# Chunks 4 to 15 of the first FFN layer as one stage for the first three units, with another order of weight loads

## The chip, the cores and the metric

One core of a Trainium2 chip. The metric is device time in microseconds (us), the median of several runs of the whole kernel. Each run holds attention and two feed-forward layers.

## The reference, cut to what matters

Attention runs over 4 batches, 8 heads, 576 positions and head size 64, with a mask in blocks of 64. Its output is regrouped to 2304 tokens of 512 numbers, and two feed-forward layers follow:

```python
def _moe_ref(x, w_in, w_out, alpha):            # layer 1, w_in 512 x 2048, w_out 2048 x 512
    h = x @ w_in
    g = np.maximum(h, 0.0) + alpha * np.minimum(h, 0.0)
    return (g @ w_out).astype(np.float32)

def _moe2_ref(x, w_in, w_out):                  # layer 2
    h = x @ w_in
    g = np.where(h > 0.0, h, np.exp(np.minimum(h, 0.0)) - 1.0)
    return (g @ w_out).astype(np.float32)
```

The kernel is handed the weights as 64-bit numbers and makes 32-bit ones of them itself.

## The kernel before, in words

**Units and chunks.** The 2304 tokens are cut into five units: units 0 to 3 have 512 tokens, unit 4 has 256 (`UNITS`). The 2048 hidden features are 16 chunks f of 128. One step of a feed-forward layer is one unit with one chunk: `l1_h` (line 537) or `l2_h` (588) forms h with 12 matmuls (4 slices of the 512 inputs, times three products of high and low parts), the gate makes g and splits it into two parts, and `l1_y` (634) or `l2_y` (614) multiplies by `w_out` with 12 more. `l1_y` and `l2_y` run three steps behind (`lag = 3`), so between them the gate has three steps' time. `l1_y` adds into four PSUM banks m = 0 to 3 over a unit's chunks; five banks serve in turn (`ring("acc", ...)`).

**Stages.** A unit's chunks of layer 1 need not run in one go. During attention, units 0 to 2 do chunks 0 to 3 (`l1_beside`, 551), and their partial sums z go to memory (`zd`). Behind attention, the list `units` (720) gives the order: stage A does chunks 0 to 7 of units 3 and 4 and writes z; stage B does chunks 4 to 7 of units 0, 1 and 2, loads z, adds and writes it again; stage D does chunks 8 to 15 of all five units, loads z, adds, splits the sum and writes it as y (`yd`). Stage C is layer 2, all 16 chunks of each unit. A3 is unit 3 in stage A, and so on; a hand-over is the end of one unit's `l1_y` and the start of the next one's. Each stage entry loads the unit's x (`load_x1`, 504) unless the unit stays the same (B2 to D2). Stages A, B, D and C have 16, 12, 40 and 80 steps; step 0 starts at 264.4 us, and stage B starts with step 16, D with 28, C with 68.

**Weights.** A chunk's weights are two words of 512 KB, r = 0 for `w_in` and r = 1 for `w_out`. `load_w` (112) loads one into a raw buffer (2 of them) from SyncE's queue and decodes it in a chain: ScalarE (lines 127, 128), VectorE (132, 133, 137), GpSimd (142), ScalarE (152), VectorE (83, called from 145). `later` and `end_tick` (two ticks a step) set the place of each link in the order of the text: the first link comes `arrival` ticks behind the load. `w_at` (729) says at which step each word is asked for. Decoded weights live in three pools: four slots for chunks 0 to 3, four for 4 to 7, eight for 8 to 15; layer 2 takes the slots of layer 1 when their last reader is done.

**What sets the order.** In attention the order of all engines is the text's. Behind it only TensorE's is (`tc.manual_schedule(engines={ET.PE})`, line 710). The queues of ScalarE, VectorE, GpSimd and SyncE are ordered by the framework's planner on a timeline of its own (`schedule_with_timeline_sim=True`), with the order of the text as rank: an instruction can come earlier than it stands if its operands and its buffer are free there. On the chip each queue then runs in that order.

**Buffers for g and y.** `gs_tile` (511) takes turns between a pool of four (`gs`) and a late pool of four (`gsl`); a stage that writes y takes four tiles more from the same turns at each hand-over. `z_tile` (579) has two and two.

Of the kernel before, what the change touches and what calls it, by code (L numbers as in the profile page):

```python
# [10 lines left out]
F32R = mybir.dt.float32r  # L11
U32 = mybir.dt.uint32
I32 = mybir.dt.int32
AF = mybir.ActivationFunctionType
ALU = mybir.AluOpType
# [4 lines left out]
P = 128  # L20
B, H, S, D = 4, 8, 576, 64
NT, DM, DFF = 2304, 512, 2048
KC = DM // P
NF = DFF // P
FA = 4
# [11 lines left out]
def f32(ap):  # L37
    return ap.bitcast(F32)
# [3 lines left out]
def attention_moe_kernel(ctx: ExitStack, tc: tile.TileContext, qT, kT, v_a, v_b, w1, w2, alpha, out):  # L42
    nc = tc.nc
    pe, act, dve, pool_e = nc.tensor, nc.scalar, nc.vector, nc.gpsimd
# [4 lines left out]
    wraw_p = ctx.enter_context(pool("wraw", 2))  # L49
# [18 lines left out]
    def ring(name, *banks):  # L68
        rings[name] = list(banks)
# [9 lines left out]
    zd = [dram.tile([P, KC, n], F32, name=f"zd{u}") for u, n in enumerate(UNITS)]  # L79


    def low_part(eng, out, x, high):
        return {"v": dve, "p": pool_e}[eng].tensor_tensor(out=out, in0=x, in1=f32(high), op=ALU.subtract)  # L83
# [13 lines left out]
    def later(ticks, emit):  # L97
        due.setdefault(tick[0] + ticks, []).append(emit)
# [8 lines left out]
    late_pools = []  # L107
# [4 lines left out]
    def load_w(layer, f, r):  # L112
        if r == 0:
            wt[layer, f] = w_pools[min(f // 4, 2)].tile([P, 2, 2 * DM], F32R, tag="w", name="w")
        t = wt[layer, f]
        raw = wraw_p.tile([P, 2 * DM], U32, tag="wraw", name="wraw")
        nc.sync.dma_start(out=raw, in_=(w1, w2)[layer][f, :, r * DM:(r + 1) * DM].bitcast(U32))
        pairs = raw.rearrange("p (n t) -> p n t", t=2)
        low, high = pairs[:, :, 0], pairs[:, :, 1]
        units = low.bitcast(I32)  # L120
        hi, lo = (t[:, k, r * DM:(r + 1) * DM] for k in range(2))
        word = []

        def first():
            w = wraw_p.tile([P, DM], F32, tag="wword", name="wword")
            word.append(w)
            act.activation(out=w, in_=high.bitcast(F32), func=AF.Abs)  # L127
            act.activation(out=units, in_=low, func=AF.Copy, scale=2.0 ** -29)

        def bits():  # L130
            w, wi = word[0], word[0].bitcast(U32)
            dve.tensor_scalar(w, w, F64_MIN, F64_MAX, ALU.max, ALU.min)  # L132
            dve.tensor_scalar(wi, wi, 3, 0x3FFFFFF8, ALU.logical_shift_left, ALU.bitwise_and)  # L133

        def sign():
            wi = word[0].bitcast(U32)
            dve.scalar_tensor_tensor(  # L137
                out=wi, in0=high, scalar=0xC0000000, in1=wi, op0=ALU.bitwise_and, op1=ALU.bitwise_or)

        def rounded():  # L140
            w = word[0].bitcast(I32)
            pool_e.tensor_tensor(out=w, in0=w, in1=units, op=ALU.add)  # L142

        def last():
            low_part("v", lo, word[0], hi)
            ready.add((layer, f, r))
        lead = arrival[0]
        later(lead, first)
        later(lead + 1, bits)
        later(lead + 1, sign)  # L150
        later(lead + 2, rounded)
        later(lead + 3, lambda: act.copy(hi, word[0]))  # L152
        later(lead + 4, last)

    arrival = [2]
# [5 lines left out]
    def w_out(layer, f, part, lo, n):  # L161
        assert (layer, f, 1) in ready
        return wt[layer, f][:, part, DM + lo:DM + lo + n]
# [335 lines left out]

    CHUNKS = {"A": range(FA), "B": range(FA, 8), "D": range(8, NF), "C": range(NF)}

    def load_x1(u):
        x1[u] = t = xp.tile([P, 2, KC, UNITS[u]], F32R, tag="x1", name="x1")
# [5 lines left out]
    def gs_tile():  # L511
        turn[0] += 1
        if late_pools and turn[0] % 2:
            return late_pools[0].tile([P, 2, 512], F32R, tag="gsl", name="gsl", bufs=4)
        return gp.tile([P, 2, 512], F32R, tag="gs", name="gs", bufs=FA)

    def l1_gate(f, h, n, beside=False):

        neg = gp.tile([P, 512], F32, tag="neg", name="neg", bufs=1)[:, :n]
        g = gp.tile([P, 512], F32, tag="g", name="g", bufs=3)[:, :n]  # L520
        t = gs_tile()[:, :, :n]
        act.activation(out=neg, in_=h, func=AF.Relu, scale=-1.0)  # L522

        def gate():
            dve.scalar_tensor_tensor(out=g, in0=neg, scalar=beta[:, f:f + 1], in1=h, op0=ALU.mult, op1=ALU.add)  # L525
            return parts

        def parts():
            act.copy(t[:, 0, :], g)  # L529
            low_part("p", t[:, 1, :], g, t[:, 0, :])  # L530
        if beside:
            held.append(gate)
        else:
            later(1, gate())
        return t
# [10 lines left out]
    def to_z(u, m, acc):  # L546
        z = z_tile(m)[:, :UNITS[u]]
        copy("av"[m % 2], z, acc)
        nc.sync.dma_start(out=zd[u][:, m, :], in_=z)
# [29 lines left out]
    def z_tile(m):  # L579
        if m % 2 and late_pools:  # L580
            return late_pools[0].tile([P, 512], F32, tag="zl", name="zl", bufs=2)
        return gp.tile([P, 512], F32, tag="z", name="z", bufs=2)
# [26 lines left out]
    def acc_bank(m, first):  # L609
        if first:  # L610
            accs[m] = bank[take("acc")]
        return accs[m]
# [21 lines left out]
    def l1_y(kind, u, f, gs):  # L634
        n, first, last = UNITS[u], f == CHUNKS[kind][0], f == CHUNKS[kind][-1]
        if kind != "A" and first:
            for m in range(KC):
                zs[m] = z_tile(m)[:, :n]
                nc.sync.dma_start(out=zs[m], in_=zd[u][:, m, :])
        for m in range(KC):  # L640
            acc = acc_bank(m, first)[:, :n]
            for t, (wp_, gp_) in enumerate(PASSES):
                pe.matmul(acc, w_out(0, f, wp_, m * P, P), gs[:, gp_, :n],  # L643
                          start=first and t == 0, stop=last and t == 2)
            if last and kind == "A":
                to_z(u, m, acc)
            elif last:
                z = zs.pop(m)
                if kind == "B":
                    dve.tensor_tensor(out=z, in0=acc, in1=z, op=ALU.add)  # L650
                    nc.sync.dma_start(out=zd[u][:, m, :], in_=z)
                    continue
                ys = gs_tile()[:, :, :n]
                dve.tensor_tensor(out=z, in0=acc, in1=z, op=ALU.add)  # L654
                act.copy(ys[:, 0, :], z)
                low_part("vp"[m % 2], ys[:, 1, :], z, ys[:, 0, :])
                nc.sync.dma_start(out=yd[u][:, :, m, :], in_=f32(ys))
# [52 lines left out]
    with tc.manual_schedule(engines={ET.PE}):  # L710


        att.close()
        ps = ctx.enter_context(pool("ps_all", 1, space=PSUM))
        bank[:] = [ps.tile([P, 512], F32, name=f"bank{i}") for i in range(8)]
        w_pools.append(ctx.enter_context(pool("w2", NF - 8)))
        late_pools.append(ctx.enter_context(pool("late", 1)))
        ring("h", 5, 6, 7)
        ring("acc", *range(5))
        units = [("A", 3), ("A", 4)] + [("B", u) for u in range(3)] + [  # L720
            ("D", u) for u in (2, 4, 3, 0, 1)] + [("C", u) for u in (2, 3, 0, 1, 4)]
        fs = CHUNKS
        fs["A"] = range(8)
        steps = [(k, u, f) for k, u in units for f in fs[k]]
        first_of = {}
        for i, (k, u, f) in enumerate(steps):
            first_of.setdefault((k, u), i)
        lag = 3
        w_at = {}
        for i in range(16):  # L730
            f, r = divmod(i, 2)
            w_at[1 + i * 26 // 16] = 0, 8 + f, r
            w_at[first_of["D", 2] + 1 + 2 * i] = 1, f, r
            w_at[first_of["C", 2] - 4 + i] = 1, 8 + f, r
        gs = {}
        for i in range(len(steps) + lag):
            if i in w_at:
                load_w(*w_at[i])
            if i < len(steps):
                k, u, f = steps[i]  # L740
                if f == fs[k][1]:
                    n = units.index((k, u)) + 1
                    if n < len(units) and units[n] != ("D", u):
                        (load_x2 if units[n][0] == "C" else load_x1)(units[n][1])
                gs[i] = l2_h(u, f) if k == "C" else l1_gate(f, l1_h(u, f), UNITS[u])
            end_tick()
            if i >= lag:
                k, u, f = steps[i - lag]
                if k == "C":
                    l2_y(u, f, gs.pop(i - lag))  # L750
                else:
                    l1_y(k, u, f, gs.pop(i - lag))
            end_tick()
# [32 lines left out]
```

## Time and profile before

| | |
|---|---|
| median of 3 runs | 1022.64 us (1018.75 to 1023.74) |
| profiled execution, its own time | 1017.45 us |
| its span | 1015.7 us, granted clock 0.987 |
| TensorE busy | 963.5 us (95%), 5008 matmuls |
| VectorE, ScalarE, GpSimd busy | 543.4 (54%), 440.2 (43%), 337.5 us (33%) |
| moved by DMA | 116.25 MB; 64 loads of weights, median 4.1 us from issue to landing |

The profile shows one execution. In it, "busy" is the time in which an engine works on instructions; an idle time is named after what ended it. A row of the timeline merges neighbouring instructions of one kind, with the start of the first and the time to the end of the last, and the count. PE is TensorE, DVE VectorE, ACT ScalarE, POOL GpSimd, SPq SyncE's queue of DMA issues.

### The profile page before, as it was taken

The numbers are of one execution on the slowest core, as the hardware profiler recorded it, in microseconds if no ns is written. First come the engines' busy times: TensorE is split into PE (matmuls) and PEld (weight loads), VectorE is DVE, ScalarE is ACT, GpSimd is POOL, SyncE is SP. The second block draws the span as 40 slices with busy tenths as digits, with TensorE's granted clock in tenths as the row PEclk, the third lists the DMA queues.
The fourth block names the chain that finished last, engine by engine and source line by source line (L and its number), as shares of the span: only waits on it lengthen the run. The fifth ranks groups of instructions, "written<-read, shape, count | busy, mean of one in ns | idle before, by whom it ended". The sixth has DMA issues, their size and how long they took to land.

```text
span 1015.7 us, 13946 instructions
## 1 busy us (share of the span) xinstructions
PE 963.5 (95%) x5008; PEld 774.9 (76%) x5008; DVE 543.4 (54%) x1024; ACT 440.2 (43%) x985; POOL 337.5 (33%) x401
## 2 busy tenths in 40 slices
PE   6778999999997999899999999999999999999997
PEld 4456766766686877689888887888888888888896
DVE  5877667787477766743213378943333333333342
ACT  6876566776455553543323256422222222222222
POOL 4778575685354544443323353200000000000000
PEclk9999999999998999999999999999999999999999
DMA  6553433633537676564423275302102100200010
GB/s 210 164 198 136 156 86 107 219 93 122 196 106 226 194 236 217 171 200 161 149 83 125 90 234 185 114 1 84 41 1 84 42 1 1 81 3 0 1 43 21
DMA packets 61156, 116.25 MB, mean 114 GB/s; under 512 B 11552, under 2 KB 29984, under 8 KB 59936
## 3 DMA queue, kind: packets, MB, share of 16 engines
q1 hardware_dynamic: 60800, 115.11, 34.3%
q8 instruction: 39, 0.64, 0.3%
q10 hardware_dynamic: 288, 0.26, 0.1%
q14 instruction: 29, 0.24, 0.1%
HBM read 83.89 MB, written 31.46 MB: 114 GB/s over the span
## 4 chain that ended last, share of the span: by engine, by line
PE 68%; DVE 11%; DMA 9%; POOL 4%; ACT 4%; issue 2%; SPq 1%; POOLq 0%; ACTq 0%; DVEq 0%
PE bank L618 19%; PE bank L593 18%; PE bank L643 9%; PE bank L542 8%; DMA wraw<-w 6%; PE bank L417 3%; POOL wword L142 3%; PE bank L571 3%; DVE wword L137 2%; PE bank L357 2%; PE pair L270 2%; PE bank L560 2%; DVE wword L133 2%; DVE wword L132 2%; ACT wword L127 1%
## 5 line engine op out<-in xcount | busy, mean ns | idle before, releaser
L593 PE MATMUL bank<-x,w 128*128 128x512 f32 (+1 forms) x960 | 210.0, 368 | 0.0
L593 PEld LDWEIGHTS bank<-x,w 128*128 128x128 f32 x960 | 169.3, 188 | 31.2
L542 PE MATMUL bank<-x,w 128*128 128x512 f32 (+1 forms) x816 | 176.7, 367 | 1.3 <-DVE xtail L83 1.3
L542 PEld LDWEIGHTS bank<-x,w 128*128 128x128 f32 x816 | 142.7, 191 | 26.2 <-ACT xtail L423 1.4
L597 ACT ACTIVATE e<-bank 128x512 f32<-128x512 f32 (+1 forms) x80 | 44.4, 554 | 180.3 <-PE bank L593 180.3
L598 DVE TENSOR_SCALAR e<-e 128x512 f32<-128x512 f32 (+1 forms) x80 | 32.0, 400 | 168.2 <-ACT e L597 168.2
L142 POOL TENSOR_TENSOR wword<-wword,wraw 128x512 int32<-128x512 int32 x64 | 89.8, 1405 | 92.5 <-DVE wword L137 53.8
L525 DVE SCALAR_TENSOR_TENSOR g<-neg,beta,bank 128x512 f32<-128x512 f32 (+1 forms) x80 | 55.2, 689 | 100.2 <-ACT neg L522 98.9
L643 PE MATMUL bank<-gsl,w 128*128 128x512 f32 (+1 forms) x408 | 94.6, 379 | 13.7 <-ACT z L87 5.3
L618 PE MATMUL bank<-w,gsl 128*128 128x512 f32 x432 | 105.2, 390 | 0.8 <-DVE z L654 0.5
L618 PE MATMUL bank<-w,gs 128*128 128x512 f32 x432 | 104.6, 389 | 0.0
L90 POOL TENSOR_SCALAR p<-p,stat 128x128 f32<-128x128 f32 (+4 forms) x144 | 81.3, 579 | 53.9 <-DVE stat L328 43.4
L643 PEld LDWEIGHTS bank<-gsl,w 128*128 128x128 f32 x408 | 72.8, 196 | 30.0 <-DVE z L650 6.3
L618 PEld LDWEIGHTS bank<-w,gsl 128*128 128x128 f32 x432 | 80.4, 188 | 17.9 <-DVE z L654 1.0
L618 PEld LDWEIGHTS bank<-w,gs 128*128 128x128 f32 x432 | 80.6, 188 | 16.4
L319 ACT ACTIVATE p<-pair,stat 128x128 f32<-128x128 f32 (+4 forms) x144 | 78.3, 557 | 26.9 <-DVE stat L292 20.5
L643 PE MATMUL bank<-gs,w 128*128 128x512 f32 (+1 forms) x408 | 87.8, 364 | 0.0
L83 POOL TENSOR_TENSOR gs<-g,gs 128x512 fp32r<-128x512 f32 (+1 forms) x46 | 57.2, 1244 | 88.0 <-ACT gs L529 77.4
L643 PEld LDWEIGHTS bank<-gs,w 128*128 128x128 f32 x408 | 70.6, 189 | 12.2
L83 DVE TENSOR_TENSOR w<-wword,w 128x512 fp32r<-128x512 f32 x64 | 61.0, 957 | 24.5 <-ACT w L152 23.7
L522 ACT ACTIVATE neg<-bank 128x512 f32<-128x512 f32 (+1 forms) x80 | 44.2, 552 | 68.2 <-PE bank L542 67.0
L292 DVE TENSOR_REDUCE stat<-pair 128x2 f32<-128x256 f32 (+3 forms) x80 | 63.2, 806 | 5.9 <-PE pair L275 3.8
(82 smaller groups left out, 1256.1 us busy)
## 6 DMA issues: line engine op xcount, KB each, us to landing
wraw<-w SPq DMA_DIRECT2D x64, 512.0 KB, 4.1
x<-xd SPq DMA_DIRECT2D x24, 512.0 KB, 7.7
xd<-x SPq DMA_DIRECT2D x4, 2048.0 KB, 8.7
x<-yd SPq DMA_DIRECT2D x4, 2048.0 KB, 8.3
vraw<-v_a SPq DMA_DIRECT2D x24, 256.0 KB, 3.6
zd<-z SPq DMA_DIRECT2D x20, 256.0 KB, 3.2
kraw<-kT SPq DMA_DIRECT2D x16, 288.0 KB, 4.3
yd<-gs SPq DMA_DIRECT2D x8, 512.0 KB, 3.2
```

The source lines that it names most:

```text
L83: return {"v": dve, "p": pool_e}[eng].tensor_tensor(out=out, in0=x, in1=f32(high), op=ALU.subtract)
L90: return pool_e.tensor_scalar(out, x, 1.0 if scale is None else scale, 1.0, ALU.mult, ALU.mult)
L142: pool_e.tensor_tensor(out=w, in0=w, in1=units, op=ALU.add)
L292: peak = lambda out, x, axis=AX.X: dve.tensor_reduce(out=out, in_=x, axis=axis, op=ALU.max, negate=True)
L319: act.activation(out=out, in_=x, func=AF.Exp, bias=stat[:, k:k + 1], accum_out=stat[:, SUMS + 2 * k:SUMS + 2 * k + 1])
L522: act.activation(out=neg, in_=h, func=AF.Relu, scale=-1.0)
L525: dve.scalar_tensor_tensor(out=g, in0=neg, scalar=beta[:, f:f + 1], in1=h, op0=ALU.mult, op1=ALU.add)
L542: pe.matmul(h, w_in(0, f, wp_, kc), x[:, xp_, kc, :n], start=kc == 0 and t == 0, stop=kc == KC - 1 and t == 2)
L593: pe.matmul(h, w_in(1, f, wp_, kc), x[:, xp_, kc, :], start=kc == 0 and t == 0, stop=kc == KC - 1 and t == 2)
L597: act.activation(out=e, in_=h, func=AF.Exp)
L618: pe.matmul(acc, gs[:, gp_, tg * P:(tg + 1) * P], w_out(1, f, wp_, 0, DM), start=f == 0 and t == 0, stop=f == NF - 1 and t == 2)
L643: pe.matmul(acc, w_out(0, f, wp_, m * P, P), gs[:, gp_, :n], start=first and t == 0, stop=last and t == 2)
```

## The change

- Stage B takes chunks 4 to 15 (`CHUNKS["B"]`) and writes y as D does; stage D is left with units 4 and 3. The order is A3, A4, B2, B0, B1, D4, D3, then C for units 2, 0, 1, 3, 4. The number of steps stays: 16, 36, 16 and 80.
- `w_at` has a written list of steps for the words of layer 1's chunks 8 to 15, `w_in` words ahead of their `w_out` words (sorted by 3r + f). Words of layer 2's chunks 0 to 3 are asked for from B0's first step (28) on, every two steps; those of chunks 4 to 7 from step 48 on, when unit 1 has used layer 1's chunks 4 to 7; those of 8 to 15 as before.
- The first link of decoding stands 4 ticks (two steps) behind the load instead of 2, up to step 63.
- Raw buffers: 3 instead of 2. The late pool for g: 3 instead of 4.

```diff
--- before.py
+++ after.py
@@ -113,7 +113,7 @@
         if r == 0:
             wt[layer, f] = w_pools[min(f // 4, 2)].tile([P, 2, 2 * DM], F32R, tag="w", name="w")
         t = wt[layer, f]
-        raw = wraw_p.tile([P, 2 * DM], U32, tag="wraw", name="wraw")
+        raw = wraw_p.tile([P, 2 * DM], U32, tag="wraw", name="wraw", bufs=3)
         nc.sync.dma_start(out=raw, in_=(w1, w2)[layer][f, :, r * DM:(r + 1) * DM].bitcast(U32))
         pairs = raw.rearrange("p (n t) -> p n t", t=2)
         low, high = pairs[:, :, 0], pairs[:, :, 1]
@@ -499,7 +499,7 @@
 
 
 
-    CHUNKS = {"A": range(FA), "B": range(FA, 8), "D": range(8, NF), "C": range(NF)}
+    CHUNKS = {"A": range(8), "B": range(FA, NF), "D": range(8, NF), "C": range(NF)}
 
     def load_x1(u):
         x1[u] = t = xp.tile([P, 2, KC, UNITS[u]], F32R, tag="x1", name="x1")
@@ -511,7 +511,7 @@
     def gs_tile():
         turn[0] += 1
         if late_pools and turn[0] % 2:
-            return late_pools[0].tile([P, 2, 512], F32R, tag="gsl", name="gsl", bufs=4)
+            return late_pools[0].tile([P, 2, 512], F32R, tag="gsl", name="gsl", bufs=3)
         return gp.tile([P, 2, 512], F32R, tag="gs", name="gs", bufs=FA)
 
     def l1_gate(f, h, n, beside=False):
@@ -646,10 +646,6 @@
                 to_z(u, m, acc)
             elif last:
                 z = zs.pop(m)
-                if kind == "B":
-                    dve.tensor_tensor(out=z, in0=acc, in1=z, op=ALU.add)
-                    nc.sync.dma_start(out=zd[u][:, m, :], in_=z)
-                    continue
                 ys = gs_tile()[:, :, :n]
                 dve.tensor_tensor(out=z, in0=acc, in1=z, op=ALU.add)
                 act.copy(ys[:, 0, :], z)
@@ -717,24 +713,25 @@
         late_pools.append(ctx.enter_context(pool("late", 1)))
         ring("h", 5, 6, 7)
         ring("acc", *range(5))
-        units = [("A", 3), ("A", 4)] + [("B", u) for u in range(3)] + [
-            ("D", u) for u in (2, 4, 3, 0, 1)] + [("C", u) for u in (2, 3, 0, 1, 4)]
+        units = [("A", 3), ("A", 4)] + [("B", u) for u in (2, 0, 1)] + [
+            ("D", u) for u in (4, 3)] + [("C", u) for u in (2, 0, 1, 3, 4)]
         fs = CHUNKS
-        fs["A"] = range(8)
         steps = [(k, u, f) for k, u in units for f in fs[k]]
         first_of = {}
         for i, (k, u, f) in enumerate(steps):
             first_of.setdefault((k, u), i)
         lag = 3
-        w_at = {}
+        words = sorted((3 * r + f, f, r) for f in range(8) for r in range(2))
+        w_at = dict(zip((1, 3, 4, 6, 7, 8, 10, 12, 14, 16, 18, 19, 21, 22, 24, 25), ((0, 8 + f, r) for _, f, r in words)))
+        freed = first_of["B", 1] + 8
         for i in range(16):
             f, r = divmod(i, 2)
-            w_at[1 + i * 26 // 16] = 0, 8 + f, r
-            w_at[first_of["D", 2] + 1 + 2 * i] = 1, f, r
+            w_at[first_of["B", 0] + 2 * i if i < 8 else freed + 2 * i - 16] = 1, f, r
             w_at[first_of["C", 2] - 4 + i] = 1, 8 + f, r
         gs = {}
         for i in range(len(steps) + lag):
             if i in w_at:
+                arrival[0] = 4 if i < first_of["C", 2] - 4 else 2
                 load_w(*w_at[i])
             if i < len(steps):
                 k, u, f = steps[i]
```

## Rows read from the trace of the kernel before

**Rows 1.** Timeline, TensorE (start, us, engine, line, operation, count) around five hand-overs.

```profile
314.76 0.52 PE L643 MATMUL bank<-gsl,w 128*128 128x256 f32 x3
324.15 2.55 PE L542 MATMUL bank<-x,w 128*128 128x256 f32 x12
326.54 1.59 PE L643 MATMUL bank<-gs,w 128*128 128x256 f32 x12
327.97 1.60 PE L542 MATMUL bank<-x,w 128*128 128x256 f32 x12
...
374.64 0.84 PE L643 MATMUL bank<-gsl,w 128*128 128x512 f32 x3
381.13 2.91 PE L542 MATMUL bank<-x,w 128*128 128x512 f32 x12
...
400.20 0.84 PE L643 MATMUL bank<-gsl,w 128*128 128x512 f32 x3
404.48 2.90 PE L542 MATMUL bank<-x,w 128*128 128x512 f32 x12
...
423.54 0.84 PE L643 MATMUL bank<-gsl,w 128*128 128x512 f32 x3
431.47 3.24 PE L542 MATMUL bank<-x,w 128*128 128x512 f32 x12
434.54 2.88 PE L643 MATMUL bank<-gs,w 128*128 128x512 f32 x12
437.26 2.88 PE L542 MATMUL bank<-x,w 128*128 128x512 f32 x12
...
626.36 1.52 PE L618 MATMUL bank<-w,gsl 128*128 128x512 f32 x6
630.49 2.89 PE L593 MATMUL bank<-x,w 128*128 128x512 f32 x12
```

**Rows 2.** Windows (busy us of each engine, granted clock, DMA share, GB/s), stage D.

```profile
454.00:591.00 137.00, 137.00 (x694) 117.20 (x694) 41.51 (x62) 43.88 (x82) 45.84 (x39) 1.00 0.41 135
```

**Rows 3.** Windows, only instructions on the decoded word (DVE, ACT, POOL; counts).

```profile
239.00:345.00 106.00, 49.67 (x69) 22.21 (x35) 24.94 (x18) 0.97 0.57 184
345.00:455.00 110.00, 52.89 (x71) 21.68 (x34) 25.48 (x18) 0.97 0.61 199
455.00:587.00 132.00, 0.58 (x1) 1.14 (x2) 0.00 (x0) 1.00 0.39 128
```

**Rows 4.** Timeline, all engines, A3 to A4 ([idle before <- what ended it]).

```profile
313.86 0.62 ACT L152 CAST w<-wword 128x512 fp32r<-128x512 f32 x1 [2.03 <-POOL wword L142]
...
317.36 0.66 ACT L127 ACTIVATE wword<-wraw 128x512 f32<-128x512 f32 x1 [1.32 <-DMA wraw<-w]
...
319.98 0.59 ACT L87 COPY z<-bank 128x512 f32<-128x512 f32 x1
...
320.63 1.01 PE L643 MATMUL bank<-gsl,w 128*128 128x256 f32 x3 [5.35 <-ACT z L87]
```

**Rows 5.** Waits of ScalarE, 301 to 337 us (total, times, longest).

```profile
ACT w L152 <- POOL wword L142: 6.8, 3, 2.9
...
ACT wword L127 <- DMA wraw<-w: 2.8, 2, 1.4
ACT wraw L128 <- DMA wraw<-w: 2.1, 1, 2.1
```

**Rows 6.** Waits of the load queue, 264 to 460 us.

```profile
SPq L117 <- POOL wword L142: 79.9, 30, 5.8
```

**Rows 7.** Timeline, VectorE and GpSimd at A3 to A4.

```profile
315.13 0.47 DVE L525 SCALAR_TENSOR_TENSOR g<-neg,beta,bank 128x256 f32<-128x256 f32 x1
...
318.51 0.43 DVE L133 TENSOR_SCALAR wword<-wword 128x512 uint32<-128x512 uint32 x1
...
319.89 1.29 POOL L142 TENSOR_TENSOR wword<-wword,wraw 128x512 int32<-128x512 int32 x1 [3.05 <-ACT wraw L128]
...
320.04 1.43 DVE L133 TENSOR_SCALAR wword<-wword 128x512 uint32<-128x512 uint32 x1
```

## The prediction, made before the change was run

> **What bounds the kernel now.** I read the summary first: TensorE is busy 95% of the span, so what can be won is the time it loses. Then I read its timeline from the end of attention to the second layer, looking for steps longer than normal. A normal full step is twelve matmuls for `l1_h` and twelve for `l1_y`; twelve take 437.26 - 434.54 = 2.72 us, and 1.43 us on the half-size unit 4 [rows 1]. Six places are longer, all where a unit's last `l1_y` hands its accumulators over:
>
> - A3 to A4: the `l1_y` that starts at 314.76 should give way at 316.19; it does at 324.15, and the twelve after it take 2.39 instead of some 1.44: 7.96 + 0.95 = 8.9 us.
> - A4 to B0: 1.0 us, the same pattern as the next (its two rows, at 351.90 and 355.60, are 3.70 apart).
> - B0 to B1: 381.13 - 374.64 - 2.72 = 3.8 us.
> - B1 to B2: 404.48 - 400.20 - 2.72 = 1.6 us.
> - B2 to D2: 431.47 - 423.54 - 2.72 = 5.2, and 0.35 in the slow twelve after it: 5.6 us.
> - D1 to C2: 630.49 - 626.36 - 2.72 = 1.4 us.
>
> Sum 22.3 us. The reader is to see what the D stage does in the same view: from 454 to 591 TensorE is busy 137.00 of 137 us with a granted clock of 1.00, the 2.4 GHz level [rows 2], although four units hand over there, each with a copy and a split per accumulator that stage B doesn't have. So the hand-over itself is free. The view that counts the decoding tells the two stretches apart: 18 words were decoded on GpSimd from 239 to 345, 18 from 345 to 455, none from 455 to 587 [rows 3]. A word takes 106/18 = 5.9 us and later 110/18 = 6.1. The five large stalls lie inside the decoding.
>
> How decoding reaches TensorE is read at A3 to A4 [rows 4]: ScalarE waited 2.03 us for GpSimd, then 1.32 us for a load of weights; its queue is in order, so the copy of the first accumulator ran only at 319.98, and TensorE, idle 5.35 us, went on at 320.63. From 301 to 337 ScalarE waited 6.8 us for GpSimd's word and 2.8 + 2.1 = 4.9 us for loads [rows 5]. The load's own queue waited 79.9 us, 30 times, until GpSimd had finished with a raw buffer [rows 6].
>
> **One fact decides how the change is read.** The kernel before asks for layer 2's first 16 words at steps 29 to 59, two steps apart, so up to 626.36 - 12.5 x 5.44 = 558 us. They were decoded by 455 [rows 3]. The planner orders SyncE, ScalarE, VectorE and GpSimd by its own timeline: a load goes when its tile and a raw buffer are free, and `w_at` is only a rank. So I cost the new numbers in `w_at` and the two-step lead at little (between 0 and the 4.9 us of load waits above; the buffer already claims these), and look at which tiles are free when.
>
> **Part by part.**
>
> - *One stage f 4 to 15 for units 2, 0, 1.* The matmuls are the same: three stages of 4 and three of 8 steps become three of 12. Hand-overs fall from ten before stage C (A 2, B 3, D 5) to seven (A 2, B 3, D 2). Gone are 12 stores and 12 loads of z (256 KB each) and the x of two units (8 x 512 KB): 12 x 2 x 0.256 + 8 x 0.512 = 10.3 MB of 116. The 12 additions of z on VectorE lie beside matmuls when nothing delays them; worth nothing alone.
> - *Where decoding falls.* Slots of f 0 to 3 come free in A4 as before, those of f 4 to 7 only after unit 1's step for f 7, at step 46 instead of 27. So 24 words remain in the dense stretch instead of 32: at 6.1 us a word, from 239 to 239 + 146 = 385. With the A stalls of below, the end of unit 2 (its last `l1_y`, step 30) comes at 404.48 + 2 x 5.44, less the stalls ahead of it that go (3.7 at A3 to A4, and the 3.8 and 1.6 inside), some 406. That is 20 us after the last of the 24 words. The other 8 words run from step 43 to 46, about 475 to 490, plus 8 x 6.1 us at the longest: 539 us; B1 to D4 (step 54, about 535) is at their edge. B0 to B1 (step 42) and D4 to D3 (62) lie clear.
> - *Weights are wanted sooner*: f 8 at step 20, f 15 at step 27 instead of 28 and 35. In the trace step 24 starts at 381.13, so step 27 at 381.13 + 3 x 5.44 = 397, and at 382 if every stall ahead of it went. All 16 words of layer 1 were decoded by 345 (18 in rows 3, at most one of them attention's). Slack 37 us; cost nothing. If it were gone, the price is a step of 5.4 us per late word.
> - *Third raw buffer.* A load can start one word (6 us) earlier, against a median landing of 4.1 us (the profile's DMA issues). So of ScalarE's waits at A3 to A4 the load's part goes, 4.9 of 11.7 us [rows 5], and GpSimd's stays. In proportion the 8.9 us become 8.9 x 6.8/11.7 = 5.2. Ends: 0 (as in stage D) and 8.9 (GpSimd alone holds it); I take 5.2, since the row has both waits.
> - *`gsl` with 3 buffers instead of 4.* At each of the five hand-overs that write y, the fourth split needs the buffer that the next step's `l1_y` still reads, so it waits up to 2.72 + 2.72 us. Behind it on ScalarE stand the next step's relu and split. They have the lag of three steps, 16 us, and the accumulator has been freed by then, by VectorE's addition. Cost nothing; without that cover up to 5 x 5.4 = 27 us.
>
> Sum of what is left: A3 to A4 5.2; A4 to B2 1.0 as now; B2 to B0 1.0 (between 0, stage D, and 5.6, the worst of B; decoding should be over, so nearer to 0); B0 to B1 and D4 to D3 0; B1 to D4 0.5 (0 to 5.6, likewise); D3 to C2 1.4. Together 9.1 against 22.3: 13.2 us gained. Against the profiled execution's 1017.45 us (its span 1015.7) that is 1004.3. That execution lies 5.2 us under the median of the runs, 1022.64; on the median the forecast is **1009.4 us**.
>
> **A rule against the change.** VectorE's mask took 0.43 us at 318.51 and 1.43 at 320.04, with GpSimd's 1.29 us addition running from 319.89 [rows 7]. The Trainium skill's GPSIMD Engine Reference (section 1, Specifications) says that GpSimd shares its SBUF interfaces with VectorE, which contend where VectorE works in a two-port mode or on two SBUF inputs; the trace agrees. By that rule words that come faster make one another slower, which is the last rival.
>
> **Rivals.**
>
> 1. *All stalls of layer 1 go* but D3 to C2: 1.4 left, 20.9 us gained, 1001.7. For: stage D. Against: A3 to A4 has 6.8 us of GpSimd waits that no buffer touches.
> 2. *The loss moves along.* Decoding isn't over at step 30, and 8 words meet B1 to D4: 8.9 + 1.0 + 5.6 + 3.8 + 1.4 = 20.7, 1.6 gained, 1021.0, no change. For: y's copies and splits then add to the queues at these places. Against: 24 words at 6.1 us end at 385. That the spacing in `w_at` isn't followed is part of this case: the loads still come as fast as buffers allow.
> 3. *Slower: the third buffer packs A4 too full.* A4's steps are 2.87 us. A word costs VectorE 52.89/18 = 2.94 us [rows 3] and the gate 0.47 [rows 7]. At one word a step that is 3.41, 0.54 too much, 4.3 us over eight steps; were GpSimd's 25.48/18 = 1.42 never beside it, 4.83, so 15.7 us. I take 10. It decides above 2.40/2.94 = 0.8 words a step (0.55 at the other end); now it is 2.87/5.9 = 0.49. The words of layer 2 are then squeezed in as well and A's loss stays: 8.9 + 10 + 1.0 + 5.6 + 3.8 + 1.4 = 30.7, 8.4 more than now, 1031.0.
>
> **Numbers.** 0.5% of the median, 5 us, is what a measurement of this kernel tells from no change: faster is under 1017.5, slower over 1027.8. Forecast with its own spread (1004 to 1015) 0.52; all gone 0.15; moved along 0.20; slower 0.13, in which I count the 27 us of `gsl`. Faster is the first two and a little of the third: 0.70; same 0.18; slower 0.12. For 8 in 10 the range goes from below rival 1 to just past rival 2: 1000 to 1023.
>
> **What would show it.** Right: no decoding from some 390 to 475, TensorE unbroken at B2 to B0 and B0 to B1, f 15's words decoded before 380, and a shorter idle time at A3 to A4 with ScalarE waiting for GpSimd but no longer for loads. Wrong: idle time at B2 to B0 with VectorE's z named, that is, decoding later than 24 x 6.1 us; a matmul that waits for a weight tile; A4's steps over 2.9 us one after another (rival 3); ScalarE's split of y waiting for a buffer, and TensorE for ScalarE behind it.

## The result, and the profile after

The changed kernel takes 1011.19 us (median of 5 runs, 1009.74 to 1012.03) against 1022.46 (5 runs, 1018.59 to 1023.74): ratio 0.9898, interval 0.988 to 0.9916. The forecast was 1009.4. The profiled execution has a span of 1009.4 us against 1015.7; the two spans differ by 6.3 us only, the medians by 11.3, because the profiled execution of before was itself 5 us under its median.

TensorE's timeline after the change, around the unit ends that answer to [rows 1]:

```profile
317.19 0.52 PE L643 MATMUL bank<-gsl,w 128*128 128x256 f32 x3
322.83 1.01 PE L643 MATMUL bank<-gsl,w 128*128 128x256 f32 x3 [5.12 <-ACT z L87]
...
326.04 2.76 PE L542 MATMUL bank<-x,w 128*128 128x256 f32 x12
328.60 2.29 PE L643 MATMUL bank<-gs,w 128*128 128x256 f32 x12
330.73 1.60 PE L542 MATMUL bank<-x,w 128*128 128x256 f32 x12
...
354.66 1.68 PE L643 MATMUL bank<-gsl,w 128*128 128x512 f32 x6
...
358.77 2.88 PE L542 MATMUL bank<-x,w 128*128 128x512 f32 x12
...
421.33 2.88 PE L643 MATMUL bank<-gsl,w 128*128 128x512 f32 x12
424.05 2.88 PE L542 MATMUL bank<-x,w 128*128 128x512 f32 x12
...
618.59 0.84 PE L618 MATMUL bank<-w,gsl 128*128 128x512 f32 x3
...
624.21 2.90 PE L593 MATMUL bank<-x,w 128*128 128x512 f32 x12
626.96 2.88 PE L618 MATMUL bank<-w,gs 128*128 128x512 f32 x12
```

A3 to A4: the `l1_y` at 317.19 should end at 318.62; the next twelve start at 326.04, take 2.56 and are followed by twelve that take 2.13 us instead of 1.43: 7.42 + 1.12 + 0.70 = 9.2 us. A4 to B2: 358.77 - 354.66 - 2.72 = 1.4. B2 to B0, where unit 0's first `l1_y` at 421.33 is followed by 424.05, exactly 2.72 later, loses nothing; nor do B0 to B1 (486.61), B1 to D4 and D4 to D3. D3 to C2: 624.21 - 618.59 - 2.72 = 2.9. The sum is 13.5 against 22.3.

The decoding, in the view of [rows 3]:

```profile
239.00:345.00 106.00, 58.92 (x77) 24.77 (x39) 27.03 (x20) 0.95 0.57 185
345.00:390.00 45.00, 24.87 (x31) 8.93 (x14) 12.37 (x9) 1.00 0.53 181
390.00:455.00 65.00, 0.00 (x0) 0.00 (x0) 0.00 (x0) 1.00 0.24 81
455.00:475.00 20.00, 0.00 (x0) 0.00 (x0) 0.00 (x0) 1.00 0.18 53
475.00:545.00 70.00, 26.09 (x32) 9.99 (x16) 11.49 (x8) 1.00 0.41 136
```

The reader is to see the hole: 20 words and 9 up to 390 (one that crosses an edge counts on both sides), none from 390 to 475, then 8. The hole is even longer than these edges: the last addition on GpSimd starts at 380.7, and the first link of the next eight words runs at 492.2. So it holds the ends of units 2 (421.33) and 0 (486.61). Moved by DMA are 105.76 MB instead of 116.25: 10.5 MB less, against 10.3 in the prediction, which counted a KB as 1000 bytes.

ScalarE at the end of A3, as in [rows 4], and its waits from 301 to 337, as in [rows 5]:

```profile
317.66 0.62 ACT L152 CAST w<-wword 128x512 fp32r<-128x512 f32 x1 [2.83 <-POOL wword L142]
...
319.61 0.66 ACT L127 ACTIVATE wword<-wraw 128x512 f32<-128x512 f32 x1
320.17 0.66 ACT L128 ACTIVATE wraw<-wraw 128x512 int32<-128x512 uint32 x1
321.36 0.67 ACT L128 ACTIVATE wraw<-wraw 128x512 int32<-128x512 uint32 x1 [0.54 <-DMA wraw<-w]
321.93 0.37 ACT L522 ACTIVATE neg<-bank 128x256 f32<-128x256 f32 x1
322.19 0.58 ACT L87 COPY z<-bank 128x512 f32<-128x512 f32 x1
```

```profile
ACT w L152 <- POOL wword L142: 3.7, 5, 2.8
ACT wword L127 <- DVE w L83: 3.5, 3, 2.4
ACT wraw L128 <- DMA wraw<-w: 3.3, 4, 2.0
```

The waits for GpSimd fell from 6.8 to 3.7 us and those for loads from 4.9 to 3.3. But a wait of 3.5 us is new: ScalarE's first link writes one of two word buffers, and now it waits until VectorE's last link has read it. So ScalarE's waits in the decoding are 10.5 us together, against 11.7 before. The copy of the first accumulator runs at 322.19, 5.0 us behind the start of the `l1_y`, as late as before (5.2): from 317.66 on, a cast, line 127 of two words and line 128 of three stand ahead of it in the queue.

### The profile page after: what moved, and what is told of

Its sections match the earlier page's. It is cut to its first block, busy times and chain, and to the rows that moved or that the text cites. A ratio compares the mean times of both kernels' runs of the same rounds, so it can differ in the third digit from the quotient of the medians.

```text
span 1009.4 us, 13780 instructions
## 1 busy us (share of the span) xinstructions
PE 960.8 (95%) x5008; PEld 774.3 (77%) x5008; DVE 545.4 (54%) x1012; ACT 442.0 (44%) x985; POOL 341.5 (34%) x401
## 2 busy tenths in 40 slices
DMA packets 55524, 105.76 MB, mean 105 GB/s; under 512 B 11040, under 2 KB 29472, under 8 KB 54304
## 4 chain that ended last, share of the span: by engine, by line
PE 60%; DVE 7%; DMA 2%; ACT 2%; issue 2%; POOL 1%; SPq 0%; ACTq 0%; POOLq 0%; DVEq 0%
PE bank L618 19%; PE bank L593 18%; PE bank L643 11%; PE bank L542 11%; DVE w L83 2%; DVE wword L137 2%; DVE wword L132 1%; DVE wword L133 1%; DMA wraw<-w 1%; ACT wword L127 1%; DMA xd<-xtail 1%; POOL wword L142 1%; ACT w L152 1%; DVE g L525 1%; ACT wraw L128 0%
## 5 line engine op out<-in xcount | busy, mean ns | idle before, releaser
L142 POOL TENSOR_TENSOR wword<-wword,wraw 128x512 int32<-128x512 int32 x64 | 92.7, 1449 | 76.7 <-DVE wword L137 17.1
L643 PE MATMUL bank<-gsl,w 128*128 128x512 f32 (+1 forms) x408 | 90.2, 369 | 8.3 <-ACT z L87 5.1
L643 PEld LDWEIGHTS bank<-gsl,w 128*128 128x128 f32 x408 | 71.4, 192 | 22.3 <-ACT z L87 5.6
L83 DVE TENSOR_TENSOR w<-wword,w 128x512 fp32r<-128x512 f32 x64 | 58.6, 920 | 16.5 <-ACT w L152 16.0
```

Source lines behind the costliest of these rows:

```text
L643: pe.matmul(acc, w_out(0, f, wp_, m * P, P), gs[:, gp_, :n], start=first and t == 0, stop=last and t == 2)
```

## The experiments

**One word on the theory.** The prediction held that decoding which meets a unit end makes the stalls. Runs e1 to e4 take the change apart, e5 and e10 test this on the kernel before, and e6, e7 and e9 look at A3 to A4, the stall that is left.

*e1, two raw buffers.*

```diff
-        raw = wraw_p.tile([P, 2 * DM], U32, tag="wraw", name="wraw", bufs=3)
+        raw = wraw_p.tile([P, 2 * DM], U32, tag="wraw", name="wraw")
```

> The changed kernel with two raw buffers instead of three. Theory (the gain is that unit ends no longer meet decoding; the third buffer is no part of it): 1011 us, within 3; the unit ends B2 to B0, B0 to B1 and B1 to D4 stay without idle time, A3 to A4 keeps some 9 us. Rival (the third buffer carries part of the gain): 1014 to 1017 us, with idle time back at B2 to B0 and ScalarE waiting longer for loads.

Measured: 1009.93 us (1009.54 to 1010.29), ratio 0.9904 (0.9876 to 0.9932). TensorE loses 9.0 us at A3 to A4 (4.5 of it waiting for ScalarE's z) and nothing at B2 to B0, B0 to B1 and B1 to D4. As the theory had it: the third buffer is no part of the gain.

*e2, the two-step lead taken back.*

```diff
-                arrival[0] = 4 if i < first_of["C", 2] - 4 else 2
+                arrival[0] = 2
```

> The changed kernel with the first link of decoding 2 ticks behind the load instead of 4. Theory (what is written outside TensorE's order is only a rank): 1011 us, within 1.5, the same stalls at the same places. Rival (the two-step lead keeps ScalarE from waiting for loads): 1014 or more, with ScalarE's waits for loads longer by 10 us or more in 264 to 460.

Measured: 1012.84 us (1011.75 to 1014.18), ratio 0.9926 (0.9906 to 0.9945). The order of instructions on ScalarE, VectorE, GpSimd and SyncE is the same as in the changed kernel, so this is the same program twice: the lead is a rank that decided nothing, and 1.7 us is what two such medians can differ by (the 1.5 expected was too narrow). The two traces of this one program also differ at single unit ends: A3 to A4 loses 7.7 us here and 9.2 in the changed kernel, D3 to C2 4.2 and 2.9.

*e4, the merged stage alone.* Two raw buffers, four late g buffers, lead 2 and the old list:

```diff
-        w_at = dict(zip((1, 3, 4, 6, 7, 8, 10, 12, 14, 16, 18, 19, 21, 22, 24, 25), ((0, 8 + f, r) for _, f, r in words)))
+        w_at = {1 + i * 26 // 16: (0, 8 + i // 2, i % 2) for i in range(16)}
```

> The merged stage alone: the changed kernel with two raw buffers, four late g buffers, the old lead and the old list of steps for layer 1's words. Theory: the merge carries all of the gain, 1011 to 1013 us. Rival (the parts are needed together): 1016 or more, with idle time at B2 to B0 or at a weight tile.

Measured: 1007.17 us (1006.44 to 1011.68), ratio 0.9886 (0.9851 to 0.9921). That is under the 1011 to 1013 expected, and less than the changed kernel in its median: the merge carries the whole gain.

*e3 and e4 again, on one chip.* e3 is the changed kernel with the old list, so it differs from e4 by the third raw buffer, the late g buffer given for it, and the lead.

> The changed kernel with the old list of steps for layer 1's words (three raw buffers, three late g buffers and the two-step lead stay). It differs from the merged stage alone by the third raw buffer with its late g buffer, since the lead changed nothing. Theory (the third raw buffer lets decoding run denser through the end of A3 and of D3 and costs some 3 us): 1010 to 1013 us, with 2 us or more lost at D3 to C2. Rival (the new list costs it): 1007 to 1008.

> The merged stage alone once more, beside the other two on one chip. If the third raw buffer costs something, it is 2 us or more below e3_oldlist in these runs; else within 1 us of it.

Measured: e3 1013.04 us (1010.99 to 1014.47), ratio 0.9924 (0.9905 to 0.9943); e4 1008.61 (1008.35 to 1008.85), ratio 0.988 (0.9861 to 0.9899). The two intervals don't meet: buffer 3, with its g buffer, costs 4.4 us. The windows of the decoding from 300 to 345 show how, first e3, then e4:

```profile
300.00:345.00 45.00, 34.29 (x45) 14.50 (x23) 15.46 (x11) 0.92 0.63 211
```

```profile
300.00:345.00 45.00, 26.96 (x39) 11.58 (x19) 13.42 (x9) 0.96 0.60 197
```

11 words on GpSimd against 9. The other traces agree: 12 in the changed kernel and in e2, with three raw buffers, and 10 in e1 and in the first run of e4, with two. And TensorE's waits behind 264 us, e3 first:

```profile
PE bank L643 <- ACT z L87: 5.8, 2, 4.4
PE bank L643 <- DVE zl L89: 2.7, 2, 1.8
PE bank L618 <- DVE z L650: 1.9, 1, 1.9
```

```profile
PE bank L643 <- ACT z L87: 3.2, 1, 3.2
PE bank L643 <- DVE zl L89: 1.8, 2, 1.0
```

In these two traces A3's and A4's ends pay more in e3, and D3 to C2 has a wait of 1.9 us that e4 doesn't have. Only the last is clear of what traces of one program differ by: D3 to C2 loses 3.7 us in e3, 2.9 and 4.2 in the changed kernel and e2, and 0.3 and 0.5 in the two runs of e4. At A3 to A4 e3 loses 9.0 us and e4 6.3 here, but 8.4 in its first run. The raw buffer's share is read from e1 and e2, which ran on one chip and differ by it and by the lead, which decided nothing: 1009.93 against 1012.84 us, ranges that don't meet, 2.9 us. The g buffer wasn't measured alone.

*e5, the kernel before with layer 2's words held to their steps.* A copy of one column on GpSimd writes the raw buffer ahead of the load and reads the g of the step before:

```diff
+        if behind is not None:
+            copy("p", raw[:, :1].bitcast(F32), f32(behind[:, 1, :1]))
         nc.sync.dma_start(out=raw, in_=(w1, w2)[layer][f, :, r * DM:(r + 1) * DM].bitcast(U32))
...
-                load_w(*w_at[i])
+                load_w(*w_at[i], behind=gs[i - 1] if first_of["D", 2] < i < first_of["C", 2] - 4 else None)
```

> The kernel before, its stages unchanged; each of layer 2's first 16 words is held back by a small GpSimd copy into its raw buffer that reads the g of the step before, so that the load goes at the step that the list names (29 to 59) and not earlier. Theory (decoding that meets the unit ends of B makes the stalls, not the number of unit ends): the losses at B0 to B1, B1 to B2 and B2 to D2, 10.9 us together, go down to under 2, and the time to 1012 to 1015, though B still has all its z traffic. Rival (B's own hand-overs, z loads and x loads make the stalls): 1021 or more, the three stalls still 8 us or more together.

Measured: 1020.97 us (1018.01 to 1021.85), ratio 0.9998 (0.9979 to 1.0017): no change. The windows (columns as in [rows 2]) say why:

```profile
345.00:455.00 110.00, 110.00 (x515) 92.24 (x514) 32.70 (x52) 32.94 (x58) 35.62 (x32) 1.00 0.45 146
455.00:600.00 145.00, 136.81 (x662) 114.49 (x661) 75.50 (x115) 64.21 (x119) 70.06 (x63) 0.98 0.54 181
```

B, the first row, has no idle time left, with all its z and x traffic: that half of the theory stands. But stage D, which lost nothing in [rows 2], now idles for 145.00 - 136.81 = 8.2 us. One word each two steps was enough to stall three of the four unit ends in this window: with the slow twelve behind them, D2 to D4, D4 to D3 and D3 to D0 lose 1.9, 2.7 and 7.4 us, together the 12.0 that the four ends of A4 and B lost before; D0 to D1 loses nothing. The time missed its mark because the stalls moved with the words. The largest is not one of many words in the queue, but of a single one that is late (D3 to D0, where the load was issued at 530.66):

```profile
534.98 0.66 ACT L129 ACTIVATE wword<-wraw 128x512 f32<-128x512 f32 x1 [5.49 <-DMA wraw<-w]
...
535.67 0.43 DVE L134 TENSOR_SCALAR wword<-wword 128x512 f32<-128x512 f32 x1 [5.41 <-ACT wword L129]
...
537.21 0.68 DVE L656 TENSOR_TENSOR z<-bank,z 128x512 f32<-128x512 f32 x1
...
537.94 0.96 PE L645 MATMUL bank<-gsl,w 128*128 128x512 f32 x3 [2.12 <-DVE z L656]
```

ScalarE stands idle for the load, VectorE for ScalarE's link, and the addition that frees the accumulator comes behind both. Part of e5's loss is thus the price of holding a load back.

*e10, the same, with the words in groups between D's unit ends.*

```diff
-            w_at[first_of["D", 2] + 1 + 2 * i] = 1, f, r
+            w_at[31 + 8 * (i // 4) + i % 4] = 1, f, r
```

> The kernel before, stages unchanged; layer 2's first 16 words are held back as in e5, but in groups of four that lie between the unit ends of stage D (steps 31 to 34, 39 to 42, 47 to 50, 55 to 58; the ends are at 38, 46, 54, 62). Theory: the stalls in B vanish as in e5, and D loses under 3 us instead of 9, so 1010 to 1014 us without any merging. Rival (decoding beside stages that end often costs the time wherever it lies): 1018 or more.

Measured: 1009.73 us (1008.85 to 1010.89), ratio 0.9895 (0.9873 to 0.9917).

```profile
345.00:455.00 110.00, 110.00 (x514) 92.23 (x514) 35.57 (x56) 33.47 (x60) 35.46 (x32) 1.00 0.44 143
455.00:600.00 145.00, 145.00 (x714) 123.20 (x714) 88.08 (x127) 71.11 (x128) 76.43 (x67) 1.00 0.58 195
```

Same stages, same words, same number of unit ends, now without idle time from 345 to 600. It gains as much as the change, without merging anything. D's last end, D1 to C2, lies behind this window in the decoding of layer 2's last words; it loses 5.1 us (1.4 before). What counts, by these cases, is whether links of the decoding that still wait stand ahead of the work that frees the accumulators; a word as such need not cost anything. One was being decoded at D4 to D3 here (its first link at 479.77, the `l1_y` at 485.63), where ScalarE had waited 1.49 us for the load, and nothing was lost.

*e6, A4 behind B2*, on e4, so that A3's end meets the dense decoding with full steps behind it:

```diff
-        units = [("A", 3), ("A", 4)] + [("B", u) for u in (2, 0, 1)] + [
+        units = [("A", 3), ("B", 2), ("A", 4), ("B", 0), ("B", 1)] + [
```

> The merged stage alone (two raw buffers, four late g buffers, old lead) with the units in the order A3, B2, A4, B0, B1, D4, D3, so that layer 1's last words are decoded in steps of 5.4 us and not in unit 4's of 2.9 us; layer 1's words are ranked at steps 1 to 16. Theory (what is left at A3 to A4, 9 us, comes from decoding in the short steps): A3 to B2 loses about as much as an end in stage B before, 1.6 to 5.6 us, B2 to A4 and A4 to B0 under 1 each, and the time is 1001 to 1004 us. Rival (a unit end in the dense decoding costs the same wherever it lies, or layer 1's words come too late for the earlier B2): 1007 us or more.

Measured: 1008.53 us (1007.34 to 1011.37), ratio 0.9884 (0.9861 to 0.9906), e4's time. TensorE at A3 to B2:

```profile
320.55 0.84 PE L643 MATMUL bank<-gsl,w 128*128 128x512 f32 x3
325.40 0.97 PE L643 MATMUL bank<-gsl,w 128*128 128x512 f32 x3 [4.01 <-ACT z L87]
327.24 2.93 PE L643 MATMUL bank<-gsl,w 128*128 128x512 f32 x6 [0.87 <-DVE zl L89]
329.96 4.47 PE L542 MATMUL bank<-x,w 128*128 128x512 f32 x12
334.27 2.91 PE L643 MATMUL bank<-gs,w 128*128 128x512 f32 x12
```

329.96 - 320.55 - 2.72 = 6.7 us, and 4.31 - 2.72 = 1.6 in the slow twelve behind: 8.3 us, as with unit 4 (8.4 and 6.3 in the two runs of e4). A4 to B0 loses 1.7, also over the 1 expected. My reason, A4's short steps, falls; the rival was right. A unit end in the dense decoding costs the same with long steps.

*e7, a lighter decoding.* The clamp, shift and mask of the words of layer 1's chunks 8 to 15 are left out:

```diff
         def bits():
             w, wi = word[0], word[0].bitcast(U32)
+            if layer == 0 and f >= 8:
+                return
```

> The changed kernel without VectorE's first two operations (clamp, shift and mask) on layer 1's words of chunks 8 to 15: part of the decoding is left out, so its weights are not the reference's. Theory (VectorE, slowed by GpSimd on decoding, is what A3's end waits for): VectorE is busy under 75% from 300 to 337, and the loss at A3 to A4 falls from 9 to 4 us or less. Rival (ScalarE's waits in the chain make it, whatever VectorE does): 7 us or more stay.

Measured, one run: 1013.91 us. VectorE is busy 30.06 of 37 us from 300 to 337 (81%; 88% in the changed kernel), and the loss at A3 to A4 is 324.68 - 317.07 - 1.43 = 6.2 us, 0.4 more behind it. VectorE isn't under 75%, and the loss is neither 4 or less nor 7 or more: unclear as a verdict. Decoding on ScalarE went up, from 6.90 us in 11 instructions to 9.29 in 15 between 300 and 325 (changed kernel, then e7):

```profile
300.00:325.00 25.00, 18.70 (x24) 6.90 (x11) 9.23 (x7) 0.90 0.65 202
```

```profile
300.00:325.00 25.00, 15.07 (x15) 9.29 (x15) 9.86 (x7) 0.94 0.69 235
```

GpSimd has 7 words in both of these windows, but from 270 to 317, the end of A3 in both, 12 against 9. A cheaper link was answered by more words. What A3 to A4 saved was lost again at A4 to B2: 6.8 us instead of 1.4.

*e9, a gap at A3's end.* e4, with layer 1's words held at the steps below and layer 2's first eight at 31 to 38, by e5's copy:

```diff
+        held_to = (1, 2, 3, 4, 5, 6, 12, 13, 15, 17, 18, 19, 20, 21, 22, 24)
+        w_at = dict(zip(held_to, ((0, 8 + f, r) for _, f, r in words)))
...
+            w_at[first_of["B", 0] + 3 + i if i < 8 else freed + 2 * i - 16] = 1, f, r
...
+                load_w(*w_at[i], behind=gs[i - 1] if i < first_of["B", 1] else None)
```

> The merged stage alone, and each word of layer 1's chunks 8 to 15 and of layer 2's chunks 0 to 3 held back by a GpSimd copy that reads the g of the step before. The steps leave a gap at the end of A3: words at steps 1 to 6, the next at 12; layer 2's first eight at steps 31 to 38, behind the end of B2. Theory (a unit end loses time where decoding is in ScalarE's and VectorE's queues ahead of the copies of its accumulators): A3 to A4 falls from 8 to 9 us to under 3, and the time to 1001 to 1004 us. Rival (that end is short of cover because A4's matmuls are short, whatever is decoded): 7 us or more stay there and the time is 1007 or more.

Measured: 1001.83 us (999.22 to 1003.15), ratio 0.9823 (0.9804 to 0.9842). It beats both kernels. Windows from 300 to 337, changed kernel first, then e9:

```profile
300.00:337.00 37.00, 31.12 (x188) 28.56 (x188) 32.64 (x47) 23.69 (x46) 21.08 (x17) 0.86 0.66 213
```

```profile
300.00:337.00 37.00, 37.00 (x249) 34.25 (x248) 18.13 (x27) 15.90 (x33) 15.12 (x19) 1.00 0.56 179
```

TensorE goes from 31.12 of 37 us at a granted clock of 0.86 to 37.00 at 1.00, the 2.4 GHz level. The timeline shows the cause: the copies of A3's accumulators, of which the first came at 322.19, now wait for TensorE and not TensorE for them:

```profile
312.06 0.59 ACT L87 COPY z<-bank 128x512 f32<-128x512 f32 x1 [0.25 <-PE bank L645]
...
313.44 0.59 ACT L87 COPY z<-bank 128x512 f32<-128x512 f32 x1 [0.48 <-PE bank L645]
...
315.35 1.60 PE L645 MATMUL bank<-gsl,w 128*128 128x256 f32 x12
316.79 1.60 PE L544 MATMUL bank<-x,w 128*128 128x256 f32 x12
```

The `l1_y` at A3 to A4 gives way after 316.79 - 315.35 = 1.44 us: nothing is lost, though A4's matmuls are as short as ever. A4 to B2 and B0 to B1, where words are being decoded, still lose 1.7 and 1.3 us.

## Why the prediction was right, and where not

**Right in the main:** the merge takes the unit ends of B out of the decoding. Forecast: the last of 24 words at 385, no decoding until 475, B2 to B0 and B0 to B1 free, eight words behind; the trace has these. e5 and e10 show that it is this, and not the fewer hand-overs or the smaller traffic: B with all its unit ends and z traffic has no idle time there.

**Luck in the 385.** Two errors offset each other. From 239 to 382 the trace has 28 additions on GpSimd and not 24: the last two of attention's 16 words come first, and two words of layer 2's chunk 4 go that far ahead of their slot and are cast only at 490.11. And a word took 143/28 = 5.1 us, not 6.1.

**Luck in the 1009.4.** The stalls behind 279 us shrank by 8.8 us in the two traces and not by 13.2. The medians differ by 11.3, because the profiled execution of before was itself 5 us under its median.

**The term that was mis-sized is A3 to A4**, 5.2 us forecast and 9.2 measured. Its step reads "of ScalarE's waits at A3 to A4 the load's part goes" through the third raw buffer. The load's waits did shrink, but a wait for the word buffer took their place, ScalarE's waits went from 11.7 to 10.5 us only, and more words came in the same time. So the copies came as late as before. With two raw buffers e1 loses 9.0 us there and e4 8.4 and 6.3: the third buffer gains nothing at this end. Over the whole kernel it costs 2.9 us (e1 against e2), with its g buffer 4.4 (e3 against e4). More words at a time is where the last rival starts, but its sign isn't there: A4's steps take 333.61 - 330.73 = 2.88 us again.

The rule of the Trainium skill that stood beside it (GPSIMD Engine Reference, section 1, Specifications: VectorE, in a two-port mode or with two SBUF inputs, contends with GpSimd for the SBUF interfaces that they share) has a part here that stays open. VectorE's time for a word from 239 to 345 rose from 49.67/18 = 2.76 to 58.92/20 = 2.95 us, the way the rule has it. At D3 to C2 the addition of z waits behind a clamp (line 132) that took 1.51 us beside a GpSimd addition of 1.51; the clamp before it, at 616.77, took 0.43. e7, with two of VectorE's operations gone, still lost 6.6 us at A3 to A4, but its verdict is unclear.

**The other terms:** A4 to B2 1.4 for 1.0; B2 to B0 none for 1.0; B1 to D4 none for 0.5; D3 to C2 2.9 for 1.4. What is missing in the spans (8.8 us gained behind 279, 6.3 in all) lies at the start. TensorE before, then after:

```profile
264.40 11.16 PE L542 MATMUL bank<-x,w 128*128 128x512 f32 x48 [1.27 <-DVE xtail L83]
...
279.02 2.88 PE L542 MATMUL bank<-x,w 128*128 128x512 f32 x12
```

```profile
265.52 11.30 PE L542 MATMUL bank<-x,w 128*128 128x512 f32 x48 [1.27 <-DVE xtail L83]
277.50 0.50 PE L643 MATMUL bank<-gsl,w 128*128 128x512 f32 x1 [0.67 <-ACT gsl L529]
...
281.45 2.88 PE L542 MATMUL bank<-x,w 128*128 128x512 f32 x12
```

The first step starts 1.1 us later and the four steps up to the first full alternation take 15.9 instead of 14.6. No term stood for this, and the change needn't be its cause: e5 and e10, whose text is that of the kernel before up to there, start at 265.61 and 266.03 and take 17.7 and 17.5 us. The trace of before has a short start.

**Costed at nothing, and rightly:** the earlier need of the weights (no matmul waits for a weight tile), the lead (e2: same order), and the numbers of `w_at` as spacing. The three late g buffers cost TensorE no wait at B2, B0, B1 and D4, but were not tried alone, and at D3 to C2 a part of theirs isn't ruled out: e1, with three of them and two raw buffers, loses 2.0 us there, e4 0.3 and 0.5.

## What to carry to other kernels

Find out which stalls lie inside a burst of side work, and move the burst or the hand-over so that they don't meet: here that was worth 12 to 14 us by merging stages (e4), 11 us by grouping loads (e10), and 19 us by merging and a gap (e9). Where a planner orders the queues, a step number is only a rank; here a data dependence held a load back, at the price that engines wait for it if it is late. A further buffer for side work didn't relieve the engines that the side work shares with the main chain: it let more of it in.

## What had not been expected of the hardware

In each kernel four hand-overs with copy and split run free where no words are decoded (D2 to D1 before, B2 to D3 after), and one word each two steps already leaves 8.2 us idle over D's unit ends (e5), 4.9 of it behind one late word. After each long stall the next twelve half-size matmuls took 2.39 us before and 2.56 after the change instead of 1.44: from 325 to 331, behind the stall at A3 to A4, the changed kernel has a granted clock of 0.57. e9, without a stall there, has 1.00 from 300 to 337, where the changed kernel has 0.86.
